# Output products summed over all heads in column tiles, their sums turned by VectorE out of PSUM

## The chip, the cores and the metric

The kernel runs on one core of a Trainium2 chip. The metric is the device time of one execution in microseconds; the time before is the median of three runs. TensorE (PE in the profile) multiplies, VectorE (DVE), ScalarE (ACT) and GpSimd (POOL) work on the results, and SyncE (SP) and GpSimd issue the DMA transfers.

## What is computed

A layer and all of its gradients. The rows x (2048 x 512) are normalized to xn; one branch is a recurrent attention over 64 segments of 32 rows, the other a dense layer with a squared ReLU. Cut to what matters here:

```python
for s in range(n_seg):                        # 64 segments
    h = concatenate([mem, xn[s]])             # 8 memory rows + 32 rows
    q, k, v = h @ Wq, h @ Wk, h @ Wv          # 32 heads of 128
    p = softmax(where(mask, q @ k.T * scale, -1e9))
    o = sum over heads of (p @ v) @ Wo        # 40 x 512
    mem = o[:8]                               # the next segment's memory
    outs.append(o[8:])
out = x + concatenate(outs) + dense(xn)
```

The outputs are `out` and, by the chain rule from `grad_out`, the gradients of x, the first memory, the four attention weights and the dense layer's parameters. The memory makes two chains: forward, segment after segment, and backward, from the last to the first.

## The kernel before

It runs in stages: the dense branch forward and backward with the normalization, the projections of the "left" rows, the forward chain, the attention gradients of the left rows together with weight gradients of the dense branch, the backward chain, and the weight gradients of the attention with the last input gradients. A step of a chain works on the 8 memory rows and the first 24 rows of a segment (32 rows in all); the other 8 rows of each segment, which feed no memory, are gathered over four segments into blocks of 32 "left" rows. There are 64 steps and 16 blocks.

TensorE's array is used in column tiles: four products of 32 columns of weights each (`tile_position=(0, 32 * g)`) stand beside each other, one for each of four groups of 8 heads. `proj` (L392) makes q, k and v so, `scores` (L432 for the mask, which is added by a product of the identity with `maskA`, and L437 for q k) and `outer` (L547, four row tiles) the attention itself, and `gather` (L460) the output: for every head a product of its 32 rows with 512 columns of Wo, summed over the 8 heads of a group into 32 of the 128 partitions of `ps_R`. The backward chain uses `gather` three times a step, with the gradients of v, k and q and the turned weights. Left rows have the same products: `G0` and `G1` forward (`ps_RL`), and `G0` to `I3` backward (L1166).

The sums over the four groups are still missing then. `ra` and `rb` copy `ps_R` to SBUF as float32 (one half on VectorE, one on ScalarE), `ta` and `tb` turn it by four TensorE products with a float32 identity (`turn_ops`, L469, into `ps_sum`), and reductions on VectorE add up the groups (`over_groups`, L482): `HT` writes the 8 memory rows as the next step's input (X forward, GT backward), `xt` the other rows to XT. For left rows `left_sums` (L476) does that. `flip` (L165) turns q and k, or the gradient of the output, by whole 128x128 transposes, and `left_rows` (L350) projects left rows of later blocks with full 128-column weights.

The order of all this is written out by hand. `F_ORDER` and `B_ORDER` are lists of short names, one string for each of the four steps of a block; `play` calls them in that order, and each engine gets its instructions in the order of these calls. A name with `L.` belongs to the left rows of a block; `+` and `-` move a name to the step (or block) before or after. `ENGS` says which engine a copy runs on. PSUM tiles of a chain come from four banks in turn (`big`, `tr`), and four more banks hold the `outer` results.

Of the kernel before, what the change touches and what calls it, by code (L numbers as in the profile page):

```python
# [12 lines left out]
P = 128  # L13
# [13 lines left out]
def kernel(  # L27
# [75 lines left out]
    HG = 4  # L103
# [247 lines left out]

    def keep_left(dN, q, t, g):

        dma(S_NL[4 * q:4 * q + 4, 32 * g:32 * g + 32, t, :].rearrange("b r c -> r b c"), dN[:])
# [68 lines left out]

    def kgr(ps):
        return ps[:].rearrange("p (k g r) -> p k g r", k=4, g=HG)

    def scores(sc, qT, kTs, h, mask):

        sc3 = sc[:, 0:4 * KW].rearrange("p (k n) -> p k n", k=4)
        if mask is not None:  # L430
            w = sum(n for _, n in kTs)
            nc.tensor.matmul(sc3[:, :, 0:w], lhsT=ident[:], rhs=mask[:, :, 0:w], start=True, stop=False, skip_group_check=True)  # L432
        for k in range(4):
            c = 0
            for kT, n in kTs:
                for g in range(HG):
                    nc.tensor.matmul(sc3[32 * g:32 * g + 32, k, c:c + n], lhsT=qT[:, 4 * h + k, g, :],  # L437
                                     rhs=kT[:, 4 * h + k, g, :], start=(mask is None), stop=True,
                                     tile_position=(0, 32 * g), skip_group_check=True)
                c += n  # L440
# [11 lines left out]

    def gather(R, XT, W, h, first, last):

        for k in range(4 * h, 4 * h + 4):
            for g in range(HG):
                x, o = W(g * KH + k), R[32 * g:32 * g + 32, :]
                if len(x.shape) == 3:
                    o = o.rearrange("p (a b) -> p a b", b=P)
                nc.tensor.matmul(o, lhsT=XT(k, g), rhs=x,  # L460
                                 start=(first and k == 4 * h), stop=(last and k == 4 * h + 3),
                                 tile_position=(0, 32 * g))

    def turn_ops(o, alloc, R4, st):

        def tT(c):
            if "T" not in st:
                st["T"] = alloc("ps_sum")
            nc.tensor.transpose(st["T"][:, c * P:(c + 1) * P], R4()[:, c * P:(c + 1) * P], identF[:])  # L469
        for h in range(2):  # L470
            o["t%s" % "ab"[h]] = lambda h=h: [tT(c) for c in (2 * h, 2 * h + 1)]

    def left_sums(XT, T):

        for c in range(DC):
            nc.vector.tensor_reduce(XT[:, c], T[:, c * P:(c + 1) * P].rearrange("p (g j t) -> p j t g", g=HG, j=SPB),  # L476
                                    axis=AX.X, op=ALU.add)

    def over_groups(out, T, rows):

        with nc.allow_low_precision(reason="summed in float32, rounded once on the way out"):
            nc.vector.tensor_reduce(out, T[:].rearrange("p (c g r) -> p c r g", c=DC, g=HG)[:, :, rows], axis=AX.X,  # L482
                                    op=ALU.add)
# [97 lines left out]
    def play(order, n, steps, lefts, step, blk, done=None):  # L581
# [22 lines left out]
        "tb ta L.E0 HT",  # L604
        "L.W1 L.ob0 L.out- k0mm L.oa0 L.oa1 L.ob1 q0mm soP- L.E1 q1mm k0ev k1mm q0ev k0fl xt- q1ev k1ev k0Te q0fl "
        "q0Te q1fl k1fl k1Te L.hs s0 mx0 sb0 q1Te s1 v0mm mx1 sb1 ex0 v0ev su0 rc0 pm0 L.lq+ L.lp ex1 tu0 v1mm "
        "soN- su1 L.otr rc1 pm1 tu1 w0 v1ev ob0 L.P2 oa0 L.X0 w1 L.lo ob1 g0 oa1 g1 soP rb L.P3 km L.t3 ra tb ta "
        "soN HT",
        "k1mm q0mm k0mm L.E3 L.E2 kl L.sx- xt- q0ev k1ev q1mm k0ev k0fl q0fl q1ev k0Te L.hl++ k1fl q0Te L.u3 k1Te "
        "q1fl s0 mx0 q1Te s1 sb0 mx1 sb1 ex0 L.ldL+ ex1 su0 rc0 pm0 tu0 v0mm su1 v0ev rc1 pm1 v1mm L.X1 w0 v1ev "  # L610
        "tu1 oa0 ld L.G1 w1 soV- ob0 L.t2 km ob1 oa1 L.mtr g0 g1 ra L.P5 soP rb L.E5 tb ta HT",
        "L.G0 k0mm xt- L.ra q0mm kl q1mm k1mm k0ev q0ev k0fl q1ev k1ev q0fl k0Te q1fl q0Te k1fl L.u2 s0 q1Te "
        "L.lv+ L.lb k1Te L.t1 L.ta s1 mx0 sb0 mx1 sb1 v0mm ex0 ex1 v0ev v1mm su0 rc0 pm0 v1ev L.mst L.tb tu0 su1 "
        "w0 rc1 ob0 L.P4 pm1 tu1 L.xt oa0 L.E4 w1 oa1 soV- soN- g0 ob1 g1 km rb soV ra kl+ L.S0+ tb ta L.X2 soP "
        "L.u1 HT xt L.mx0+ L.S1+ L.sb0+ k0mm+ L.mx1+ q0mm+ L.sb1+ k1mm+ q1mm+ q0ev+ k0ev+ k1ev+ ld q1ev+ soN "
        "L.ex0+ k0fl+ q0fl+ k1fl+ k0Te+ q1fl+ q0Te+ L.ex1+ q1Te+ k1Te+ s0+ mx0+ v0mm+ sb0+ L.t0 L.su1+ ex0+ L.lm+ "
        "su0+ km+ s1+ mx1+ sb1+ v0ev+ ex1+ v1mm+ L.P0+ rc0+ v1ev+ pm0+ tu0+ ld++ w0+ oa0+ su1+ rc1+ pm1+ ob0+ "
        "L.P1+ tu1+ w1+ ld+ ob1+ L.su0+ L.rc0+ L.pm0+ oa1+ L.u0 L.rc1+ g0+ L.pm1+ g1+ soV+ L.tu0+ rb+ L.tu1+ "
        "L.W0+ L.BT ra+ kl++")
    ENGS = on_engines(  # L620
        "L.E1 L.E2 L.E4 L.oa0 L.ob0 k0ev k1ev oa0 ob0 ob1 q1Te q1ev rb v0ev v1ev",
        "L.E0 L.E3 L.E5 L.oa1 L.ob1 L.pm0 L.pm1 L.ra k0Te k1Te oa1 pm0 pm1 q0Te q0ev ra")
    with sb("fw", 1) as fw, psum("fr", 4) as fr, psum("fpp", 1) as fpp, \
# [64 lines left out]
        def left(b):  # L688
# [27 lines left out]
            for p in range(2):  # L716
                def S_(p=p):
                    ps["s%d" % p] = big("ps_scL")
                    scores(ps["s%d" % p], B_["qL"], ((B_["kM"], NL), (B_["kL"], NL)), p, maskL)
# [26 lines left out]
            def ra():  # L746
                st["R4"] = fo.tile([P, D], F32, name="R4L", tag="R4s")
                ENGS["L.ra"](st["R4"][:], ps["R"][:])
            o["ra"] = ra
            turn_ops(o, big, lambda: st["R4"], st)  # L750
            o["xt"] = lambda: left_sums(B_["XT"][:, :, :, 0:M], st["T"])

# [5 lines left out]
            for i in range(PER):  # L758
# [5 lines left out]
                def P_(i=i, q=q, t=t, g=g, h=h):  # L764
                    ps["L", i] = big("ps_L")
                    left_rows(ps["L", i], lambda dc: XL1[:, dc, (q - 1) * P:q * P], t, g, h)
# [39 lines left out]
        def fwd(s):  # L806
# [30 lines left out]
            for t, u, n in ((1, 2, "k"), (0, 1, "q"), (2, 0, "v")):  # L837
                for p in range(2):
# [10 lines left out]
                    def fl_(n=n, p=p, u=u):  # L849
                        ps[n, p] = tr("ps_tr")  # L850
                        flip(ps[n, p], T["N"][:, u, HC[p]])
# [5 lines left out]
            for p in range(2):  # L857
                def S_(p=p):
                    ps["s", p] = big("ps_sc")
                    scores(ps["s", p], T["qT"], ((T["kT"], L),), p, maskA)  # L860
# [26 lines left out]
            def ra(h):  # L887
                if "R4" not in st:
                    st["R4"] = fo.tile([P, D], F32, name="R4", tag="R4s")
                c = slice(h * 2 * P, (h + 1) * 2 * P)  # L890
                ENGS["r%s" % "ab"[h]](st["R4"][:, c], ps["R"][:, c])
            o["ra"], o["rb"] = lambda: ra(0), lambda: ra(1)
            turn_ops(o, big, lambda: st["R4"], st)

            def HTf():
                if s + 1 < NSEG:
                    b1, j1 = divmod(s + 1, SPB)
                    over_groups(block(b1)["X"][:, :, j1 * SEG:j1 * SEG + M], st["T"], slice(0, M))
            o["HT"] = HTf
            o["xt"] = lambda: over_groups(B_["XT"][:, :, j, M:SEG], st["T"], slice(M, SEG))  # L900
# [12 lines left out]
        with tc.manual_schedule():  # L913
# [9 lines left out]
            after_o = {"L.ra": 6, "L.tb": 5, "L.xt": 5}  # L923
# [13 lines left out]
    with sb("la", 2) as la, sb("ls", 2) as ls, sb("lo", 1) as lo_, sb("wg", 2) as wg, psum("lpp", 1) as lpp, psum("lr", 4) as lr:  # L937
# [151 lines left out]
        "L.ko1 kg0 d41 qea0 L.G2 qeb0 tu1 qg0 kla0 qp1 klb0 L.I1 qea1 qeb1 kp1 qg1 keb1 kea1 klb1 kg1 rb ra L.H1 "  # L1089
        "tb kla1 vtr ta ldq HT",  # L1090
        "L.H2 o0mm L.ra1 vc- pb- o0ev o1mm L.ktr o0fl o0te o1ev vp0 ldk- xt- s0 L.kst d10 d20 vea vp1 d30 vla "
        "o1fl d40 vtr vlb vg0 veb kp0 vc tu0 vtr+ o1te ldp qp0 qeb0 s1 qea0 d11 d21 kea0 keb0 d31 vg1 qg0 kla0 "
        "klb0 d41 kg0 kp1 tu1 kea1 qp1 L.I3 keb1 qeb1 kg1 qea1 qg1 rb ra L.I2 L.vtr tb ta HT",
        "L.G3 o0mm ldn- ldk- L.ra2 o0ev kla1- o1mm o1ev ldp o0fl pb- xt- klb1- vp0 o0te s0 vea L.gs d10 vp1 vla "
        "d20 ldq- o1fl d30 d40 vlb vg0 kp0 veb tu0 o1te keb0 qp0 s1 qea0 klb0 vg1 kea0 kla0 pb d11 d21 kg0 L.sl- "
        "d31 vc d41 tu1 qeb0 kp1 qp1 keb1 qg0 qea1 L.gl+ kea1 kg1 qeb1 qg1 rb ra tb ta L.H3 kla1 HT",
        "klb1- o0mm o1mm L.vst o0ev o0fl o1ev L.ra3 xt- vp0 o1fl vtr ldn- o0te o1te vp1 ldp vea s0 L.ldt+ ldq- "
        "vla d10 L.qtr s1 d20 d30 d40 vc tu0 vg0 d11 veb vlb d21 L.I0+ L.ldv+ kp0 ldk- kla0 qp0 vg1 d31 kea0 keb0 "
        "d41 kg0 qea0 qeb0 qg0 tu1 kp1 klb0 qp1 kea1 L.vo1+ qeb1 L.G0+ pb keb1 qea1 kg1 qg1 kla1 L.vo0+ rb L.ldk+ "
        "L.ta L.tb tb ra ta L.lq+ HT L.H0+ L.ra0+ L.xt o0mm+ o1mm+ o0ev+ o1ev+ o0fl+ o0te+ L.qst vp0+ o1fl+ ldq "  # L1100
        "L.qo0+ klb1 s0+ vea+ L.ko0+ o1te+ vla+ d10+ d20+ d30+ vp1+ vlb+ d40+ ldn s1+ vg0+ kp0+ ldk veb+ d11+ "
        "d21+ xt ldn+ tu0+ keb0+ d31+ ldp+ L.G1+ vg1+ L.qo1+ qp0+ L.sx+ kea0+")
    ENGS = on_engines(
        "L.ra0 kea0 keb0 keb1 kla0 kla1 o0ev o1ev qea0 qea1 qeb0 rb vea veb vla vlb",
        "kea1 klb0 klb1 o0te o1te qeb1 ra")
    with sb("bq", 1) as bq, sb("bt", 1) as bt, sb("bs", 2) as bs, sb("be", 1) as be, psum("bpp", 1) as bpp, psum("br", 4) as br:
# [17 lines left out]
        def block(b):  # L1124
            if b not in blk:
# [3 lines left out]
                          "XT": (bt, [P, DC, SPB, SEG], F32), "R4": (bt, [P, D], F32)}  # L1129
# [7 lines left out]
        def left(b):  # L1137
# [19 lines left out]
            for i in range(4):  # L1157
                for x, nm in enumerate("GHI"):
                    def G_(i=i, x=x):
# [4 lines left out]
                        for m, (W, n, k) in enumerate(jobs[6 * i + 2 * x:6 * i + 2 * x + 2]):  # L1164
                            for g in range(HG):
                                nc.tensor.matmul(ps["R", i][32 * g:32 * g + 32, :].rearrange("p (a b) -> p a b", b=P),  # L1166
# [377 lines left out]
```

## Time and profile before

| | us |
|---|---|
| median of the runs (three) | 3063.05 |
| lowest and highest | 3062.07, 3064.35 |
| span of the profiled execution, first to last instruction | 3059.8 |
| window of the forward chain, 300 to 1173 | 873; TensorE busy 807.5, DMA share 0.66 |
| window of the backward chain, 1455 to 2410 | 955; TensorE busy 858.5, DMA share 0.70 |
| float32 products of L469, busy | 102.4 + 13.8 + 10.9 |
| groups of L460 products, busy | 146.7, 141.6, 133.4 (backward), 126.4, 33.5 (forward) |

The mean granted TensorE clock of the execution is 0.971. "Busy" is the time in which at least one instruction of a group ran; products overlap, so the busy time of a group can't be had from its mean and count. "Issue" as a releaser means that the engine waited for nothing that the profile shows. A line such as `128*32 128x512 bf16` is a product with weights of 128 rows and 32 columns and 512 columns of moving data.

### The profile page before, as it was taken

What the parts mean: (1) busy time and instruction counts of PE and PEld (TensorE: products, weight loads), DVE (VectorE), ACT (ScalarE), POOL (GpSimd) and SP (SyncE); (2) the same over time, 40 slices, a digit from 0 to 9 for tenths busy, and PEclk for the clock granted to TensorE, in tenths of its full rate; (3) what the DMA queues carried; (4) which work ended last, traced back from release to release, by engine and by line L of the source; (5) the groups of instructions that cost most, each with busy time, mean ns of one, the idle gap of its engine ahead of it and who ended that gap; (6) DMA issues with size and microseconds to landing.
All of it is one profiled execution on the core that took longest, in us unless ns stands there. A gap on an engine that the chain in (4) does not pass through costs nothing. (4 is left out here: it accounts for less than half of the span.)

```text
span 3059.8 us, 109712 instructions
## 1 busy us (share of the span) xinstructions
PE 2705.4 (88%) x48600; PEld 1386.8 (45%) x48600; DVE 1319.5 (43%) x3581; ACT 994.7 (33%) x2306; POOL 658.0 (22%) x1264
## 2 busy tenths in 40 slices
PE   8997899999999886877799899998989559999998
PEld 4453444444444444446444444444444224444443
DVE  5452566666666664334345444544545201100010
ACT  2422444444444444323333333333333101111111
POOL 0000000000000000113343433434343213322222
PEclk9998999999999998999999999999999879999999
DMA  9548375766767767777577676776777899898991
GB/s 257 185 146 250 101 188 161 189 181 172 190 168 182 165 157 192 229 230 220 149 173 174 190 187 164 177 203 169 176 200 175 238 192 217 194 211 207 204 207 39
DMA packets 794559, 566.78 MB, mean 185 GB/s; under 512 B 579409, under 2 KB 681570, under 8 KB 790754
## 3 DMA queue, kind: packets, MB, share of 16 engines
q1 hardware_dynamic: 748322, 430.47, 58.8%
q0 software_dynamic: 40528, 126.53, 13.5%
q8 instruction: 381, 6.24, 0.9%
q10 hardware_dynamic: 5232, 2.75, 0.4%
q14 instruction: 96, 0.79, 0.1%
HBM read 193.61 MB, written 238.56 MB: 141 GB/s over the span
## 5 line engine op out<-in xcount | busy, mean ns | idle before, releaser
L1505 PE MATMUL ps_gw<-gn,HNc 128*128 128x512 bf16 x1920 | 416.4, 379 | 0.0
L1505 PEld LDWEIGHTS <-HNc 128*128 128x128 bf16 x1920 | 187.8, 98 | 223.9
L374 ACT CAST f_N<-ps_proj 128x512 bf16<-128x512 f32 x320 | 185.9, 581 | 243.9 <-PE ps_proj L392 223.4
L1476 ACT CAST wt<-ps_gw 128x512 bf16<-128x512 f32 x128 | 74.4, 586 | 503.5 <-PE ps_gw L1505 474.4
L392 PEld LDWEIGHTS <-X 128*32 128x32 bf16 x6144 | 153.3, 97 | 161.3 <-DVE X L482 13.9
L835 POOL COPY kM<-f_kT 128x256 bf16<-128x256 bf16 x64 | 25.6, 401 | 786.7 <-DVE f_kT L377 594.9
L1459 DVE TENSOR_TENSOR gx<-ps_rows,gb 128x512 f32<-128x512 f32 x16 | 11.1, 692 | 420.5 <-PE ps_rows L1457 418.2
L1505 PE MATMUL ps_gw<-GOc,gn 128*128 128x512 bf16 x640 | 142.2, 385 | 54.8 <-DMA GOc<-S_GM 54.8
L460 PE MATMUL ps_gR<-Wk,gk 128*32 128x512 bf16 x2048 | 146.7, 386 | 19.4 <-ACT gk L374 12.9
L392 PE MATMUL ps_proj<-Wk,X 128*32 128x512 bf16 x2048 | 135.4, 384 | 12.6 <-DVE X L482 6.9
L460 PE MATMUL ps_gR<-Wq,gq 128*32 128x512 bf16 x2048 | 141.6, 382 | 1.2 <-issue 1.2
L374 ACT CAST gk<-b_pp 128x256 bf16<-128x256 f32 x192 | 68.8, 377 | 208.3 <-PE b_pp L547 146.6
L1477 POOL DMA_DIRECT2D out_dram<-wt x128 | 69.2, 541 | 309.5 <-ACT wt L1476 309.4
L1239 POOL COPY PD<-b_P 32x320 bf16<-32x320 bf16 x256 | 114.9, 449 | 95.3 <-PE b_pp L1292 64.4
L460 PE MATMUL ps_gR<-Wv,gv 128*32 128x512 bf16 x2048 | 133.4, 379 | 0.3 <-issue 0.3
L392 PE MATMUL ps_proj<-Wo,GT 128*32 128x512 bf16 x2048 | 123.9, 384 | 7.9 <-POOL GT L1203 6.7
L392 PE MATMUL ps_proj<-Wq,X 128*32 128x512 bf16 x2048 | 128.7, 382 | 0.0
L460 PE MATMUL ps_R<-Wo,OT 128*32 128x512 bf16 x2048 | 126.4, 388 | 0.0
L469 PE MATMUL ps_sum<-identF,R 128*128 128x128 f32 x512 | 102.4, 295 | 24.6 <-ACT R L374 18.4
L392 PE MATMUL ps_proj<-Wv,X 128*32 128x512 bf16 x2048 | 124.1, 378 | 0.0
L1505 PEld LDWEIGHTS <-gn 128*128 128x128 bf16 x640 | 63.4, 99 | 132.3 <-issue 59.6
L374 ACT CAST gON<-ps_proj 128x512 bf16<-128x512 f32 x128 | 74.9, 585 | 143.2 <-PE ps_proj L392 141.5
(260 smaller groups left out, 5128.0 us busy)
## 6 DMA issues: line engine op xcount, KB each, us to landing
S_A<-f_N SPq DMA_DIRECT2D x64, 512.0 KB
out_dram<-wt POOLq DMA_DIRECT2D x142, 128.0 KB, 4.6
S_A<-f_N SPq DMA_DIRECT2D x64, 256.0 KB
S_GB<-gv SPq DMA_DIRECT2D x32, 512.0 KB
S_GB<-gq SPq DMA_DIRECT2D x32, 512.0 KB
S_GB<-gk SPq DMA_DIRECT2D x32, 512.0 KB
b_kN<-S_A POOLq DMA_DIRECT2D x63, 256.0 KB, 5.0
b_qN<-S_A POOLq DMA_DIRECT2D x63, 256.0 KB, 5.4
```

What stands on the lines that cost most here:

```text
L374: nc.scalar.copy(out, in_)
L392: nc.tensor.matmul(o, lhsT=hT[:, dc, :], rhs=x, start=(dc == 0), stop=(dc == DC - 1), tile_position=(0, 32 * g))
L460: nc.tensor.matmul(o, lhsT=XT(k, g), rhs=x, start=(first and k == 4 * h), stop=(last and k == 4 * h + 3), tile_position=(0, 32 * g))
L469: nc.tensor.transpose(st["T"][:, c * P:(c + 1) * P], R4()[:, c * P:(c + 1) * P], identF[:])
L835: o["km"] = lambda: nc.gpsimd.tensor_copy(B_["kM"][:, :, :, lc], T["kT"][:, :, :, 0:M])
L1239: nc.gpsimd.tensor_copy(PD[32 * g:32 * g + 32, g], C["P"][32 * g:32 * g + 32, :, 0:L])
L1459: nc.vector.tensor_tensor(out=gx[:], in0=ps[:], in1=gb[:], op=ALU.add)
L1476: nc.scalar.copy(wt[:], ps[:])
L1477: pdma(dst, wt[:])
L1505: nc.tensor.matmul(ps[:], lhsT=l(rc), rhs=r(rc), start=(n == 0), stop=(n == RC_ALL - 1))
```

## The change

`gather` and the left rows' products now call `columns_of`: for each head four products, each with all of the head's 32 rows and 128 of the 512 columns (32 out of every 128), on the four column tiles. All 32 heads are summed in PSUM, and `ps_R` holds 128 x 128 sums. A single 32x32-block transpose on VectorE (`RT`) brings them out of PSUM, already turned, to XT; `HT` copies the 8 memory rows from there. The copies `ra`/`rb`, the TensorE turns `ta`/`tb` and the reductions `xt`, `over_groups` and `left_sums` are gone. In the forward chain the turns of q and k (`flip_tiles`), the masks and the left projections (`left_tiles`) are done in four column tiles as well, and the mask covers only the columns that it can change. The backward flips stay whole. `HT` is a VectorE copy in both chains; in the backward chain XT has two buffers, and a memset of its memory rows is dropped.

```diff
+    def left_tiles(ps, x, t, g, h):
+        c0 = g * GW + h * 512
+        for dc in range(DC):
+            for c in range(4):
+                nc.tensor.matmul(ps[32 * c:32 * c + 32, :], lhsT=x(dc)[:, 32 * c:32 * c + 32], rhs=Wqkv[t][:, dc, c0:c0 + 512],
+                                 start=(dc == 0), stop=(dc == DC - 1), tile_position=(0, 32 * c))
...
+    def flip_tiles(ps, srcN):
+        for k in range(4):
+            for c in range(4):
+                nc.tensor.transpose(ps[32 * c:32 * c + 32, k * P:(k + 1) * P], srcN[:, k * P + 32 * c:k * P + 32 * c + 32],
+                                    ident[:], tile_position=(0, 32 * c))
...
-            w = sum(n for _, n in kTs)
-            nc.tensor.matmul(sc3[:, :, 0:w], lhsT=ident[:], rhs=mask[:, :, 0:w], start=True, stop=False, skip_group_check=True)
+            m, lo, hi = mask
+            for c in range(4):
+                nc.tensor.matmul(sc3[32 * c:32 * c + 32, :, lo:hi], lhsT=ident[:, 32 * c:32 * c + 32], rhs=m[:, :, lo:hi],
+                                 start=True, stop=False, tile_position=(0, 32 * c), skip_group_check=True)
...
+    def columns_of(R, XT, W, first, last):
+        x = W if len(W.shape) == 3 else W.rearrange("p (a b) -> p a b", b=P)
+        for c in range(HG):
+            nc.tensor.matmul(R[32 * c:32 * c + 32, 0:P].rearrange("p (a b) -> p a b", b=32), lhsT=XT,
+                             rhs=x[:, :, 32 * c:32 * c + 32], start=first, stop=last, tile_position=(0, 32 * c))
+
     def gather(R, XT, W, h, first, last):
         for k in range(4 * h, 4 * h + 4):
             for g in range(HG):
-                x, o = W(g * KH + k), R[32 * g:32 * g + 32, :]
-                if len(x.shape) == 3:
-                    o = o.rearrange("p (a b) -> p a b", b=P)
-                nc.tensor.matmul(o, lhsT=XT(k, g), rhs=x,
-                                 start=(first and k == 4 * h), stop=(last and k == 4 * h + 3),
-                                 tile_position=(0, 32 * g))
+                columns_of(R, XT(k, g), W(g * KH + k), first and k == 4 * h and g == 0, last and k == 4 * h + 3 and g == HG - 1)
...
 F_ORDER, second step (end)
-        "soN- su1 L.otr rc1 pm1 tu1 w0 v1ev ob0 L.P2 oa0 L.X0 w1 L.lo ob1 g0 oa1 g1 soP rb L.P3 km L.t3 ra tb ta "
-        "soN HT",
+        "L.otr rc1 pm1 tu1 w0 v1ev ob0 L.P2 oa0 L.X0 w1 L.lo ob1 g0 oa1 g1 soP L.P3 km L.t3 RT HT soN",
 B_ORDER, second step (end)
-        "klb0 d41 kg0 kp1 tu1 kea1 qp1 L.I3 keb1 qeb1 kg1 qea1 qg1 rb ra L.I2 L.vtr tb ta HT",
+        "kp1 tu1 kea1 qp1 L.I3 keb1 qeb1 kg1 qea1 qg1 RT HT L.I2 L.vtr",
...
+            o["RT"] = lambda: nc.vector.transpose(B_["XT"][:, :, j, :], ps["R"][:, 0:P])
             def HTf():
                 if s + 1 < NSEG:
                     b1, j1 = divmod(s + 1, SPB)
-                    over_groups(block(b1)["X"][:, :, j1 * SEG:j1 * SEG + M], st["T"], slice(0, M))
+                    ENGS["HT"](block(b1)["X"][:, :, j1 * SEG:j1 * SEG + M], B_["XT"][:, :, j, 0:M])
...
-            o["xt"] = lambda: left_sums(B_["XT"][:, :, :, 0:M], st["T"])
+            o["RT"] = lambda: nc.vector.transpose(B_["XT"][:, :, :, 0:M], ps["R"][:, 0:P])
...
-                if j == SPB - 1:
-                    nc.gpsimd.memset(B_["XT"][:, :, :, 0:M], 0.0)
```

## The prediction

> **What bounds the kernel now.** I read the page first (busy shares, then the DMA queues), then the groups by line for TensorE, then the timeline around one turn of the forward chain, then the waits of the backward stage, and last the packed trace, record by record, for what one merged line hides. The first line gives busy time, share and instructions of TensorE; the two queue lines say what one queue carries.
>
> ```profile
> PE 2705.4 (88%) x48600; PEld 1386.8 (45%) x48600; DVE 1319.5 (43%) x3581; ACT 994.7 (33%) x2306; POOL 658.0 (22%) x1264
> ...
> q8 instruction: 381, 6.24, 0.9%
> ...
> q14 instruction: 96, 0.79, 0.1%
> ```
>
> TensorE is in use nearly always, but in the two chains it isn't full. A forward step takes 13.6 us (63 distances between the L482 reductions that write X: 870 us in all) and a backward step 14.8 us. One turn of the forward chain shows where the order of dependent work stands: start, duration, engine, line.
>
> ```profile
> 395.25 1.91 PE L460 MATMUL ps_R<-Wo,OT 128*32 128x512 bf16 x32
> ...
> 397.21 0.42 DVE L377 COPY R<-ps_R 128x256 f32<-128x256 f32 x1 [1.38 <-PE ps_R L460]
> 397.73 0.37 ACT L374 COPY R<-ps_R 128x256 f32<-128x256 f32 x1 [1.90 <-DVE R L377]
> 398.15 0.42 PEld L469 LDWEIGHTS ps_sum<-identF,R 128*128 128x128 f32 x4 [0.52 <-ACT R L374]
> 398.15 0.66 PE L469 MATMUL ps_sum<-identF,R 128*128 128x128 f32 x4
> ...
> 398.85 0.29 DVE L482 TENSOR_REDUCE X<-ps_sum 128x32 bf16<-128x128 f32 x1
> ```
>
> After the last output product the sums are copied by two engines, one after the other, turned by four float32 products and reduced; only then may the next step's projections start. From the last output product's start to the first projection's the packed trace has 2.41, 2.19, 2.83 and 2.19 us for the four steps of a forward block (mean 2.41; 0.6 to 1.7 us of it is other useful work), and 2.19 us for each backward one.
>
> The second bound is easily missed. In the backward stage TensorE stops for up to 2.8 us with no releaser (waits by engine and line: us in total, times, longest):
>
> ```profile
> PEld L547 <- issue: 108.4, 209, 2.8
> ...
> PE b_pp L547 <- issue: 11.6, 5, 2.7
> ```
>
> ```profile
> 1512.93 0.18 PE L547 MATMUL b_pp<-gST,b_kN 32*128 32x32 bf16 x1
> 1515.09 0.19 PE L547 MATMUL b_pp<-gST,b_kN 32*128 32x32 bf16 x3 [1.98 <-issue]
> ```
>
> The two lines are the timeline across one of them. The stop falls in the middle of a run of equal products. In the packed trace 13 such stops in this stage, 19.1 us together, lie at one place: TensorE's own row number, counted from the start, leaves 192 or 193 when divided by 256. TensorE has 97,535 rows there and q8 brought 381 packets of 16,384 bytes, so a packet is 256 rows of 64 bytes: TensorE's program. Each packet starts only around the row where the previous block is entered (39 rows before it to 256 behind it), so just one block is on its way. In 12 of the 13 stops TensorE goes on 2.2 to 2.5 us after the latest packet's start; the packet took 0.9 to 1.2. And from the entry of a block to the start of the next packet it is, in 8 of 10 cases, 0.4 to 1.6 us (median 0.9) where the DMA engines were under 30% busy in the 2.5 us before, 0.5 to 3.4 (median 1.8) where they were over 95% busy, and 1.2 to 6.3 (median 2.95) behind the 13 stops. So a block can't be replaced in less than about 0.9 + 2.3 = 3.2 us; the shortest distance between two packets in the whole run is 3.28 us. Today a block lasts 873/145 = 6.0 us in the forward and 955/170 = 5.6 us in the backward stage (windows 300 to 1173 and 1455 to 2410 us), so the limit is seldom touched.
>
> **The change part by part.** Products, by shape. Each output product of 512 columns becomes four of 128. Four neighbours on four column tiles run together: the x32 line above is 8 such groups, (1.91 - 0.39)/7 = 217 ns a group. A group of 128 columns isn't in this trace; the nearest rows are transposes of 128 columns, 56 ns from start to start, and four-tile score products of 40 columns (L437), 25 ns a group. I take 56, which is nearest in columns; the bounds are that 25 and the 70 ns of a 160-column product (L1290). 2,560 groups of 216 become 10,240 of 56: 553 to 573 us, +8 ns per old group: +0.06 us a forward step (8 groups), +0.24 a backward step (24 of the step, 6 of the block). At 70 ns it would be 143 us more by products alone, but 256 rows would still need only 2.2 us. All 640 float32 products of L469 go (102.4 + 13.8 + 10.9 us busy), with the copies (0.42 and 0.37) and the reductions (0.29 and 0.55).
>
> The chain behind the last output product becomes: product 0.22 (mean of the 128-column transposes), hand-over 0.06, RT on DVE, hand-over 0.04, HT, hand-over 0.06. RT (float32 128x128 from PSUM, turned) has no row: between the reduction of 128x128 (0.27) and the bf16 transpose of 128x256 (0.445); I take 0.30, since it reads as many elements as the reduction. HT (32 elements) lies between the reciprocal (0.18) and the reduction (0.29): 0.20. Sum 0.87 us (0.83 to 1.10). Beside it TensorE now has, in the four forward positions, one left projection (0.92), that and L.G0 (1.83), the left scores (0.67), and W0, BT and W1 with the casts between (1.58, from the same jobs at 424.8 us). The larger of chain and cover: 0.92, 1.83, 0.87, 1.58, mean 1.30 instead of 2.41: -1.11. Without its cover a position costs 0.87. Backward, the covers are two left jobs (0.95) or one (0.88 by the chain), mean 0.92 instead of 2.19: -1.27.
>
> Flips and masks in column tiles: the stop between projection and flip (312 ns against 213 for the product alone) loses 0.10 us a step; 16 groups of 56 replace 16 transposes of 56. Between mask and score the copies of q and k end last (DVE f_qT, 0.27 us of waiting), so that drain was covered and brings nothing; at most 0.2 us in one position of four. Left projections change 4 x 216 for 4 groups of 216.
>
> The added wait is RT's for the last output product. Behind it on DVE stand HT, dN casts and L.out, or in the backward order L.xt and o0te; only HT has someone waiting (the next projection), and it is in the chain above. L.RT waits for L.G0, which is ahead of the projections anyway. No DMA is issued elsewhere; POOL loses a memset per block.
>
> So by products and chain alone: forward 13.6 - 1.11 - 0.10 + 0.06 = 12.45 us, backward 14.8 - 1.27 + 0.24 = 13.8.
>
> Program rows. Added products: 30,720 by the outputs, 3,072 by flips, 480 by masks, 792 by left projections, 640 gone: +34,424, each with its weight load, so 166,400 rows and 650 packets. Forward: +11,704 products; (37,080 + 23,408)/64 = 945 rows, 3.7 blocks a step. Backward: +22,720; (43,536 + 45,440)/64 = 1,390 rows, 5.43 blocks. Its 128-product runs ask for 256 rows in 1.8 us. The densest 128 products of this trace took 2.84 us, so that pace was never tried. The price of a block that is waited for lies between 3.2 us (above) and 2.95 + 2.4 = 5.4 us (behind the stops). The same bytes over a longer stage would lower the DMA share of the backward stage from 0.70 to about 0.5, which puts it half-way between a free queue (3.2) and a loaded one (1.8 to 2.95 plus 2.4, middle 4.7): 3.9 us.
>
> Backward every block is dense: 5.43 x 3.9 = 21.2 us, +6.4 a step, 64 steps: +410 us. Forward two of 3.7 blocks hold the 512-column projections and the softmax waits and last over 3.9 on their own; the other 1.7 need 1.7 us each, and the first of them is often already fetched, so 1.2 stops of 2.2 us: 12.45 + 2.6 = 15.1, +1.5 x 64 = +96. The rest of the span (ffn, left back, weight gradients) is untouched. 3059.8 + 506 = 3566 us of span; the median of the runs, 3063.05, is 3.2 above the span: about 3570 us.
>
> [...]
>
> **The rivals.** *The program keeps up* (0.10): packets start earlier than in this trace once rows are short, or more than one is under way. Then forward -1.15 x 64 = -74, backward -1.0 x 64 = -66: 2925 us, faster. For it: today 51 of 64 backward steps have no stop, and the densest rows of this trace never asked for more; against it: 13 stops of one kind, and never under 3.28 us between packets. It decides below 2.7 us a block, where 12.45 + 1.2 (c - 1.7) + 5.43 c equals 28.4. *Nearly* (0.07): 2.7 to 3.1 us a block, 3065 to 3225 us, typically 3120. *Loaded queue* (0.11): the median behind the stops, 5.4 us: backward 29.3 (+930), forward 3.7 x 5.4 = 20 (+410): about 4400 us. A sag of TensorE's clock would push there too: the window 2410 to 2468 us, nearly idle, shows 0.58.
>
> **How the numbers follow.** The forecast, 3.1 to 4.75 us a block, has 0.72. At 3.1: backward 16.8 (+130), forward 14.1 (+34), 3225 us; at 4.75: 25.8 (+705) and 17.6 (+256), 4025 us. With the nearest part of both neighbours the range is 3200 to 4050. About 0.2% is what a measurement of this kernel can tell from no change. Faster by more than that: the first rival and an edge of the second, 0.11; within: 0.01; slower: 0.88.
>
> **What would show it.** Right: q8 with some 650 packets, 3.5 to 4.5 us apart in the backward stage; L469 gone; stops named "issue" in the middle of output products, about 1 to 2 us each; RT near 0.30 and HT near 0.20 us. Wrong: output groups of 128 columns running at 56 ns with no stop at every 256th row, or a step under 13 us.

## The result, and the profile after

| us | before | after |
|---|---|---|
| median of the runs | 3063.7 | 3684.07 (3678.58 to 3688.45) |
| ratio | 1 | 1.203, 95% interval 1.200 to 1.205 |
| span of the profiled execution | 3059.8 | 3678.1 |
| forward chain, mean distance of steps | 13.63 | 15.89 |
| backward chain, mean distance of steps | 14.86 | 22.43 |

The 63 forward distances grew by 142.0 us in all, the 63 backward ones by 476.6, and the left rows' stage and the end by 1.3 and 0.4; the start shrank by 2.1. These add up to the 618.3 us by which the span grew, so the whole loss lies in the two chains.

The page after, busy times, granted clock (tenths in 40 slices) and the two instruction lines of the queues (packets, MB, share):

```profile
PE 2846.7 (77%) x83024; PEld 1880.6 (51%) x83024; DVE 1194.0 (32%) x3341; ACT 946.0 (26%) x2177; POOL 657.7 (18%) x1248
...
PEclk9989999999998989887788878888888877999999
...
q8 instruction: 650, 10.65, 1.2%
...
q14 instruction: 91, 0.75, 0.1%
```

TensorE is busy a little longer than before but a smaller share of the time, VectorE less, and q8 brings the 650 packets that the prediction counted. The clock is the line that its sum did not count: 0.7 and 0.8 through most of the second chain. The windows of the chains, before and after (us; busy PE, PEld, DVE, ACT, POOL; clock, DMA share, GB/s):

```profile
314.00:1173.00 859.00, 796.66 (x18328) 409.02 (x18324) 554.85 (x1593) 376.87 (x851) 50.07 (x125) 1.00 0.67 170
1458.00:2414.00 956.00, 861.52 (x21821) 440.63 (x21814) 464.37 (x1324) 343.22 (x976) 364.54 (x703) 0.99 0.70 178
```

```profile
312.00:1312.00 1000.00, 796.69 (x29752) 520.99 (x29737) 499.32 (x1470) 354.50 (x787) 50.33 (x125) 0.95 0.61 147
1599.00:3032.00 1433.00, 990.57 (x44098) 807.41 (x44099) 393.85 (x1208) 317.66 (x911) 362.78 (x687) 0.83 0.46 121
```

One turn of the backward chain after (start, duration, engine, line):

```profile
2204.64 0.66 PE L474 MATMUL ps_gR<-Wq,gq 128*32 128x128 bf16 x16
...
2205.07 1.09 PE L474 MATMUL ps_RL<-Wq,b_gqL 128*32 128x128 bf16 x32
2205.36 0.32 DVE L1315 STREAM_TRANSPOSE b_XT<-ps_gR 128x128 f32<-128x128 f32 x1 [8.86 <-PE ps_gR L474]
2205.71 0.18 DVE L385 CAST GT<-b_XT 128x32 bf16<-128x32 f32 x1
...
2205.94 2.68 PE L400 MATMUL ps_proj<-Wo,GT 128*32 128x512 bf16 x32
```

The order of dependent work is as short as it was meant to be: RT 0.32, HT 0.18, then the projection. But the 32 projection products take 2.68 us here, at a granted clock of 0.71, where 32 products of this shape took 1.91 us in the turn shown of before, at 1.00. What eats the gain stands in the waits (of the whole run: us in total, times, longest) and in the timeline across one stop:

```profile
PEld L474 <- issue: 451.4, 274, 4.7
...
PE ps_gR L474 <- issue: 257.4, 151, 4.5
...
PEld L545 <- issue: 177.1, 309, 2.8
```

```profile
2213.36 0.85 PE L474 MATMUL ps_gR<-Wv,gv 128*32 128x128 bf16 x47
2217.20 0.44 PE L474 MATMUL ps_gR<-Wv,gv 128*32 128x128 bf16 x17 [2.99 <-issue]
```

A run of 64 equal products is cut after the 47th for 2.99 us, and nothing that the profile shows released it. In the packed trace (stops of over 0.5 us, from one row's start to the next) 258 of the backward stage's 345 blocks begin with such a stop, 450.9 us in all, and 113 of the forward stage's 235, 168.5 us; nine in ten of TensorE's gaps of over 1 us lie at its row 193 modulo 256. Before, these were 14 (20.2 us) and 2 (1.3 us). So the stops grew by 431 and 167 us, where the two chains grew by 477 and 142.

### The profile page after: what moved, and what is told of

Read it like the earlier page. It is cut to its first block, busy times and chain, and to the rows that moved or that the text cites. A ratio compares the mean times of both kernels' runs of the same rounds, so it can differ in the third digit from the quotient of the medians.

```text
span 3678.1 us, 178065 instructions
## 1 busy us (share of the span) xinstructions
PE 2846.7 (77%) x83024; PEld 1880.6 (51%) x83024; DVE 1194.0 (32%) x3341; ACT 946.0 (26%) x2177; POOL 657.7 (18%) x1248
## 4 chain that ended last, share of the span: by engine, by line
PE 47%; issue 12%; DMA 3%; DVE 3%; ACT 1%; SPq 1%; POOL 0%; POOLq 0%; DVEq 0%; ACTq 0%
PE ps_gw L1474 15%; PE ps_gR L474 13%; PE ps_proj L400 5%; PE ps_RL L474 3%; PE b_pp L545 3%; PE ps_w L1029 1%; PE ps_w L1023 1%; PE ps_tr L165 1%; PE ps_sc L454 1%; PE b_pp L1272 1%; DMA wB<-S_AN 1%; DMA wB<-S_GH1N 1%; ACT gk L382 0%; DMA gn<-S_OL 0%; PE ps_R L474 0%
## 5 line engine op out<-in xcount | busy, mean ns | idle before, releaser
L474 PE MATMUL ps_gR<-Wk,gk 128*32 128x128 bf16 x8192 | 216.1, 271 | 107.8 <-issue 92.8
L474 PE MATMUL ps_gR<-Wq,gq 128*32 128x128 bf16 x8192 | 210.4, 267 | 107.9 <-issue 107.5
L400 PEld LDWEIGHTS <-X 128*32 128x32 bf16 x6144 | 175.5, 100 | 178.1 <-issue 54.3
L474 PEld LDWEIGHTS <-gk 128*32 128x32 bf16 x8192 | 180.0, 124 | 124.8 <-issue 104.8
L474 PEld LDWEIGHTS <-gq 128*32 128x32 bf16 x8192 | 178.7, 123 | 122.7 <-issue 121.4
L474 PE MATMUL ps_R<-Wo,OT 128*32 128x128 bf16 x8192 | 155.9, 236 | 68.1 <-issue 67.8
L1445 ACT CAST wt<-ps_gw 128x512 bf16<-128x512 f32 x128 | 74.5, 587 | 487.3 <-PE ps_gw L1474 478.8
L474 PE MATMUL ps_gR<-Wv,gv 128*32 128x128 bf16 x8192 | 149.2, 223 | 57.1 <-issue 57.1
L474 PEld LDWEIGHTS <-OT 128*32 128x32 bf16 x8192 | 134.7, 105 | 79.4 <-issue 77.1
L400 PE MATMUL ps_proj<-Wo,GT 128*32 128x512 bf16 x2048 | 147.7, 426 | 24.6 <-issue 12.7
L474 PEld LDWEIGHTS <-gv 128*32 128x32 bf16 x8192 | 122.1, 98 | 66.9 <-issue 63.0
```

The source lines that it names most:

```text
L400: nc.tensor.matmul(o, lhsT=hT[:, dc, :], rhs=x, start=(dc == 0), stop=(dc == DC - 1), tile_position=(0, 32 * g))
L474: nc.tensor.matmul(R[32 * c:32 * c + 32, 0:P].rearrange("p (a b) -> p a b", b=32), lhsT=XT, rhs=x[:, :, 32 * c:32 * c + 32], start=first, ...
L1445: nc.scalar.copy(wt[:], ps[:])
```

## The experiments

The theory under test is that of the prediction: TensorE's program comes in blocks of 256 rows (97,535 rows and 381 packets in the trace before, 166,382 and 650 after), a dense block can't be had in less than about 3.9 us, and the change adds rows. The rivals: the 128-column products are slow in themselves (array, PSUM, clock); the new turn or the column tiles of the turns cost the time. Steps are the mean distances in the profiled run of each kernel, as in the table.

**The new chain with the old products.**

```diff
-    for c in range(HG):
-        nc.tensor.matmul(R[32 * c:32 * c + 32, 0:P]..., rhs=x[:, :, 32 * c:32 * c + 32], ...)
+    nc.tensor.matmul(R[32 * g:32 * g + 32, :]..., rhs=x, ..., tile_position=(0, 32 * g))
```

> The changed kernel with its output products put back to one of 512 columns per head (four groups of heads on four column tiles): about 104,960 TensorE rows and 410 packets on q8 instead of 650. RT, HT, the orders, and the column tiles for forward turns, masks and left projections stay. Left out: the sum over the four groups and three quarters of the output columns. Program theory (dense blocks of 256 rows take 3.85 us): the chain's saving comes out without its price, forward steps near 12.5 us, backward steps near 13.8 us, 2920 us (2880 to 2970). Rival 'the turn on VectorE or the column tiles of the turns are what is slow': not under 3063 us. Rival 'the 128-column products are slow in themselves': as the program theory here, the next kernel tells them apart.

Measured: 2990.52 us, ratio 0.976 (0.973 to 0.980), steps 12.87 and 14.32 us, 410 packets. Its backward window:

```profile
1416.00:2338.00 922.00, 805.16 (x21508) 422.19 (x21508) 392.72 (x1214) 317.39 (x912) 362.99 (x687) 0.98 0.75 185
```

The turn, the copy and the column tiles of the turns are not what is slow: with them, and with 240 packets fewer than after, the kernel is faster than before. It is 70 us slower than was expected, and outside the range of that expectation; where this went is told below.

**The same rows, a quarter of the columns, then twice the columns.**

```diff
-            nc.tensor.matmul(R[32 * c:32 * c + 32, 0:P] ..., rhs=x[:, :, 32 * c:32 * c + 32], ...)
+            nc.tensor.matmul(R[32 * c:32 * c + 32, 0:32 * n] ..., rhs=x[:, 0:n, 32 * c:32 * c + 32], ...)   # n: 4 for the first product, then 1
...
+            nc.tensor.matmul(R[32 * c:32 * c + 32, 0:2 * P] ..., rhs=x[:, :, 64 * (c // 2):64 * (c // 2) + 64], ...)   # the second kernel
```

> The changed kernel with the same products and weight loads, 166,400 rows and 650 packets, but every output product except the first of a sum has 32 columns instead of 128 (three quarters of the columns keep only the first head: left out). Program theory: the same blocks must come, so nearly the same time, 3640 us (3580 to 3690), stops at the same row of every block and longer, since the products are shorter. Rival 'the 128-column products are slow (array time, PSUM or clock)': 10,240 groups of four at 25 ns instead of 56, so about -317 us, 3370 us or less.

> The changed kernel with every output product twice as long: 256 columns instead of 128 into twice the PSUM columns, the same 166,400 rows and 650 packets. RT reads the first 128 of the 256, which are not the wanted ones: left out is the right choice of columns. Program theory: 32 groups of 256 rows now ask for 32 x 112 = 3.6 us where a waited block takes 3.85 us, so the doubled array time fits into the stops, and the granted clock rises from 0.83 as TensorE idles less: 3690 us (3600 to 3770). Rival 'product time counts': +10,240 groups x 56 ns = +573 us, 4260 us.

Measured: 3775.05 us with 32 columns (ratio 1.233, 1.228 to 1.237), 3723.62 with 256 (1.212, 1.210 to 1.214), against 3684.07 with 128. Eight times the columns move the time by 51 us, and in the other direction. Of each kernel a group of output products (count | busy, mean ns | idle before) and the backward window, 32 columns first, then 256:

```profile
L475 PE MATMUL ps_gR<-Wq,gq 128*32 128x32 bf16 x8192 | 103.7, 192 | 197.3 <-issue 197.0
```

```profile
1635.00:3127.00 1492.00, 780.89 (x44144) 556.84 (x44146) 392.84 (x1208) 317.00 (x911) 361.36 (x686) 0.65 0.46 116
```

```profile
L475 PE MATMUL ps_gR<-Wq,gq 128*32 128x256 bf16 x8192 | 269.8, 277 | 55.4 <-issue 55.2
```

```profile
1610.00:3078.00 1468.00, 1233.36 (x44098) 1049.50 (x44095) 396.14 (x1208) 317.72 (x911) 361.99 (x686) 0.98 0.47 118
```

What the products gain in busy time, the stops take, and the other way round: TensorE is busy 781 us in one window and 1233 in the other, and the windows are 1492 and 1468 us long. The stops at block borders sum to 679 us backward with 32 columns, 450.9 with 128 and 234.3 with 256. The rival of slow products falls. So does the clock as the main cause: with 256 columns it is granted at 0.98, and the step (22.98 us) is no shorter than at 0.83 (22.43), where the slower groups are 2.2 us of array time (worked out below) against the 7.6 us by which the step grew. The kernel with 256 columns came within its expectation; the one with 32 missed it, 3775 against at most 3690. Its clock is 0.65, and its 512-column projections from GT take 601 ns in the mean, 426 in the changed kernel. The added time lies in the backward blocks without a stop, most of which hold such products: 75 of 5.2 us in the mean, against 87 of 4.5 in the changed kernel; blocks with a stop last 4.1 in both.

**Rows alone, on the kernel before.** Products of 4 columns of zeros are added to the same sums, with the old chain.

```diff
+        def zeros(k):
+            for _ in range(n):                    # n = 1, then n = 3
+                for g in range(HG):
+                    nc.tensor.matmul(R[32 * g:32 * g + 32, 0:4], lhsT=XT(k, g), rhs=zero4[:], start=False, stop=False, ...)
```

> The kernel before with one more product of 4 columns of zeros for each output product, added to the same sums (the result does not change): 118,015 rows, 461 packets. Old chain, old turns. Program theory: a stage pays only where 256 rows ask for less than 3.85 us; with 512-column products between them a group of eight products takes about 242 ns, so 256 rows take 3.9 us, just at the limit: only the array time is added, 2,560 groups of 25 ns = 64 us, 3125 us (3080 to 3220). Rival 'every added product has its price, whatever the blocks': a third of what three zeros add. Rival 'rows cost nothing': 3063 to 3127 us.

> The kernel before with three more products of 4 columns of zeros for each output product: 158,975 rows, 621 packets. Old chain, no 128-column products, no new turn. Program theory: backward 5.47 blocks a step at the 4.18 us a block that the changed kernel shows = 22.9 us (+515 us), forward 3.2 blocks, +1.5 to +2.3 us a step (+100 to +150): 3700 us (3600 to 3800), with the stops at the same row of each block, and more than three times the loss of one zero. Rivals 'columns' and 'chain': only the array time of 7,680 groups of 25 ns, +192 us at most, 3255 us.

Measured: 3248.39 us with one (ratio 1.061, 1.054 to 1.067) and 3748.99 with three (1.224, 1.213 to 1.235). Without any part of the change, three zeros cost as much as the change and more: 621 packets, steps of 15.82 and 23.72 us. Of its 347 backward blocks 222 begin with a stop, 367 us in all, at the same row of the block as after; the zeros' own array time, at most 192 us by the expectation, and the lower clock (0.87) are in the loss too and were not taken apart. The backward window, and one line of the zeros:

```profile
1599.00:3113.00 1514.00, 1145.54 (x44410) 674.51 (x44411) 459.90 (x1313) 343.19 (x974) 365.23 (x702) 0.87 0.45 115
```

```profile
L460 PE MATMUL ps_gR<-zero,gk 128*32 128x4 bf16 x6144 | 124.0, 171 | 64.4 <-issue 64.2
```

The expectation for one zero was missed, 3248 against at most 3220. It took all blocks as alike. The trace has 88 backward blocks with a stop, about 133 us or 2.1 us a step (0.3 before), where that step grew by 2.57; and the median block with a stop lasts 4.4 us, not 3.9, at a higher DMA share (0.61). So the price begins with the densest blocks and isn't a threshold of the mean: one zero costs 186 us and three 687, 3.7 times as much. That was expected to be far more uneven.

**The column tiles of the turns undone.**

```diff
-                        flip_tiles(ps[n, p], T["N"][:, u, HC[p]])
+                        flip(ps[n, p], T["N"][:, u, HC[p]])
...
-                    left_tiles(ps["L", i], ...)
+                    left_rows(ps["L", i], ...)
```

> The changed kernel with the forward turns of q and k, the masks and the left projections put back to whole products: 8,688 TensorE rows fewer (nearly all in the forward chain, 136 a step, 0.53 block), output products, RT and HT as changed. Program theory: the forward chain stops at 113 of its blocks and these rows are dense (64 products in 0.9 us), so most of 0.53 x 4.1 us comes back: -0.5 to -1.5 us a step, 3590 to 3650 us; backward unchanged at 22.4 us a step. Rival 'column tiles for the turns pay by the drain they save': +0.1 us a step, 3684 to 3695 us.

Measured: 3673.08 us, ratio to before 1.196 (1.191 to 1.200), just below the 1.203 of the changed kernel and above the expected 3590 to 3650 us. The forward step falls by 0.81 us to 15.08, as expected; the column tiles of the turns, with their 136 rows a step, cost more than the wait that they shorten: from projection to turn it was 312 ns before and 192 in the median after. But the backward step, whose code is the same and which was expected unchanged, rose from 22.43 to 23.01 us and took 37 us of it back. Its added time is in stops that end 2.1 to 3.3 us behind a packet (492.6 us against 456.0). Why the same code stops longer there stays open.

**Can the short chain be had without the rows?** First a mixture: wide products for most heads, whose sums ScalarE copies and a float32 selector (128x32, ones where the row within a group matches) adds up in PSUM, and 128-column products for the last 16, 8 or 0 heads.

```diff
+        R4 = alloc4()
+        acp(R4[:], ps["Ra"][:])                  # sums of the wide products, 128x512
+        jobs = [(XT(k, g), W(g * KH + k)) for k in range(4 * h + 4 - NC, 4 * h + 4) for g in range(HG)]
+        jobs.insert(12 if NC == 4 else len(jobs), (sel[:], R4[:]))
+        for i, (w, x) in enumerate(jobs):
+            columns_of(ps["R"], w, x, i == 0, i == len(jobs) - 1)
```

> A mixture on the kernel before: all output products but the last half of the last gather stay 512 columns wide on four groups; their sums are copied by ScalarE alone (128x512) and added over the groups by four float32 products with a 128x32 selector into the same PSUM tile as the last 16 heads, which come in 128-column products; then RT and HT as in the change. About 109,800 rows (+96 a step). Left rows, turns and masks as before. Program theory: the chain's saving seen with wide products (-0.77 us forward, -0.54 backward) less the selector (0.35) and less 0.375 block a step (0.3 to 0.8 us): between 3030 and 3110 us, 3070. Rival 'rows cost nothing, only the chain counts': 2990 to 3010 us.

> The same mixture with only the last 8 heads in 128-column products: +48 rows a step, about 103,700 rows. The ScalarE copy (0.58 us) is then not quite covered by 0.45 us of products, and the selector comes last. Program theory: the chain from the last wide product to the next projection is 2.06 us where it was 2.62, less 0.2 to 0.4 us for 0.19 block: 3020 to 3070 us, 3045. Rival 'rows cost nothing': 3000 us.

> The same mixture with no 128-column heads at all: the wide sums are copied by ScalarE alone, added and regrouped by the four selector products, turned by VectorE. No rows more than before (97,500). Program theory: no block is added, the chain behind the last output product is 0.39 + 0.06 + 0.58 + 0.04 + 0.35 + 0.06 + 0.32 + 0.03 + 0.18 + 0.05 = 2.06 us less the 0.17 that a product's end overlaps, against 2.19 to 2.41: -0.2 to -0.4 us a step, 3010 to 3040 us, 3025. Rival 'the saving came from the short chain alone, and this one is as long': 3063 us.

Measured: 3101.4 us (ratio 1.011, 1.007 to 1.014), 3081.1 (1.0025, 1.0001 to 1.0049) and 3107.17 (1.012, 1.007 to 1.016). The first is within its expectation, the second just above, the third far off. With no 128-column products TensorE waits for the copy, since the selector stands ahead of the products that covered the copies before:

```profile
2002.61 0.58 ACT L384 COPY R<-ps_gR 128x512 f32<-128x512 f32 x1 [1.78 <-PE ps_gR L520]
...
2003.25 0.43 PE L474 MATMUL ps_gR<-R,sel 128*32 128x128 f32 x8 [0.73 <-ACT R L384]
2003.34 0.57 SPq L1181 DMA_DIRECT2D S_GM<-GT  x1
2003.37 0.54 POOL L1274 DMA_DIRECT2D b_qN<-S_A  x1
...
2003.49 1.05 PE L1199 MATMUL ps_RL<-Wq,b_gqL 128*32 128x512 bf16 x16
```

The covering products of left rows start at 2003.49, behind the wait of 0.73 us. The expectation had left the queue's order out of the sum.

Then two kernels without any added product row for the chain, both on the kernel before:

```diff
-                c = slice(h * 2 * P, (h + 1) * 2 * P)
-                ENGS["r%s" % "ab"[h]](st["R4"][:, c], ps["R"][:, c])
+                c = slice(64 * h, 64 * h + 64)
+                ENGS["r%s" % "ab"[h]](st["R4"][c, :], ps["R"][h][c, :])      # two banks, copied side by side
...
+            nc.tensor.matmul(R()[0][:, c * 32:c * 32 + 32], lhsT=R4()[:, c * P:(c + 1) * P], rhs=sel[:], ...)
...
+                acp(st["R4"][:], ps["R"][:])                                 # the other kernel: one copy by ScalarE
```

> The kernel before with a shorter chain and no added row (one output tile split over two banks by head groups, so that ScalarE and VectorE copy 64 partitions each side by side, 0.69 and 0.58 us, instead of one after the other, 0.42 + 0.10 + 0.37; four float32 products with a 128x32 selector, which add up the groups, instead of four turns of 128 columns, 0.57 for 0.66; and a copy of 0.18 instead of the reduction of 0.29): the chain behind the last product 1.56 us instead of 1.93. Program theory: no block is added, so up to 0.37 us a step stays, less where useful work covers it: 3015 to 3050 us, 3030. Rival 'the chain is covered by other work or the loads end last': 3060 us. Rival 'an additional bank in the rotation of four makes steps wait': over 3070 us.

> The kernel before with the copy of the output sums done by ScalarE alone (128x512, 0.58 us) where two engines copied one half each, one after the other (0.42 + 0.10 + 0.37 us). No row, no product, no block is added. Program theory: the 0.3 us stay wherever no product covers the copy: most backward steps (cover 0.44 us or none), few forward ones (cover 0.92 us); -20 to -30 us: 3035 us (3025 to 3060). Rival 'ScalarE comes late with its other casts, or the turn of the first half now waits': 3070 us or more.

Measured: 3138.51 us (ratio 1.022, 1.020 to 1.023) and 3068.46 (0.9996, 0.998 to 1.001). In the first one the copies do run side by side, but the selector is dearer than the turns that it replaces:

```profile
2007.90 0.68 DVE L379 COPY R<-ps_gR 64x512 f32<-64x512 f32 x1 [1.09 <-PE ps_gR L462]
...
2007.99 0.58 ACT L376 COPY R<-ps_gR 64x512 f32<-64x512 f32 x1 [1.44 <-PE ps_gR L462]
...
2008.72 1.05 PE L484 MATMUL ps_gR<-sel,R 128*128 128x32 f32 x8 [0.43 <-DVE R L379]
```

Four selector products are eight in the records and take 1.05 us; the four float32 turns of 128 columns took 0.66. That is 0.39 us of the 0.7 by which the backward step grew; the rest was not followed up. The expectation (3015 to 3050 us) failed, and its rival of the additional bank, over 3070, is not excluded: no kernel tried the bank alone. In the second, which also missed its range, the chain behind the last backward product went only from 2.19 to 2.16 us. The packed trace shows why (medians, counted from that product's start, the turns in three of the four positions). The one copy ends at 1.07 us, where the second of the two had ended at 1.31. But before, two of the four turns began at 0.91, beside that second copy; now all four wait for the whole copy, and the last one begins at 1.51 instead of 1.53. That is the rival which the expectation named. No version tried here that keeps all of the sums is faster than the kernel before.

## Why the prediction was right

The forecast, slower at 3570 us within 3200 to 4050, held: 3684. Its mechanism is shown by three kernels: rows without the change bring the loss (three zeros), the change without its rows is faster than before (wide products), and the products' length hardly matters (32 and 256 columns). Step by step:

**The price of a block.** 3.9 us forecast, 3.91 measured as the median of the 258 backward blocks with a stop (3.84 if stops from 0.3 us on are counted): 1.41 us from entry to packet (about 1.5 was assumed) and 2.43 from packet to resumption (2.4). The rival of the program that keeps up falls, with its 2925 us. The prediction read the trace before a little too evenly: the 14 stops counted there now last 0.7 to 2.8 us and not all over 2, 11 of them end 2.2 to 2.5 us behind a packet and three 3.4 to 3.5, and the wait ahead of the packet is 0.6 to 3.8 us (median 3.1).

**Backward, 5.43 x 3.9 = 21.2 us.** Measured 22.43. The price was right for the typical block with a stop, but two things are missing. The blocks with a stop are uneven, and their mean is 4.08 us. And not every block is dense, as the sum had it: the 87 without a stop last 4.47 us by themselves. Each makes about half of the difference, and the mean over all 345 is 4.17, which gives 5.4 x 4.17 = 22.5. This is most of what the forecast lacked: 1.2 us x 64 = 79 us.

**Forward, 12.45 + 1.2 stops of 2.2 us.** Measured 1.77 stops a step of 1.49 us: 2.63 against 2.64, but that is luck, since more stops came and each was shorter. The base was low: 15.89 - 2.63 = 13.26 us instead of 12.45. Of these 0.8 us the groups of 128 columns can explain about half: they took 65.4 ns in the mean, 9 more than assumed, times 40 a step, 0.38 us. The rest was not traced.

**The chain.** 0.87 forecast. In the backward stage the medians are 0.22 for the product, 0.04, RT 0.317, 0.034, HT 0.182 and, at two of the four positions, 0.05 to the projection's start: 0.85. At the other two the projection waits for covers or stops. The covers held too: with wide products, 0.16 us longer than the 0.22, the four forward positions measure 1.91, 1.07, 1.93 and 1.02 us (mean 1.48; 1.30 + 0.16 was the sum), the backward ones 1.01 to 1.07 (0.92 + 0.16). Yet that kernel's backward step gained 0.54 us and not 1.15. The stall went elsewhere, which the sum had not asked: stops at block borders grew from 20.2 to 38.5 us (0.29 a step), and the waits of TensorE's weight loads for the transfer of `b_qN` from 2.8 to 19.5 us (0.26 a step). The line in the backward window before, and then in that kernel's (busy, mean ns | idle before):

```profile
L547 PEld LDWEIGHTS <-b_qN 32*128 32x128 bf16 x2048 | 37.0, 91 | 65.6 <-issue 61.0 <-DMA b_qN<-S_A 2.8
```

```profile
L545 PEld LDWEIGHTS <-b_qN 32*128 32x128 bf16 x2048 | 36.8, 91 | 76.2 <-issue 55.7 <-DMA b_qN<-S_A 19.5
```

**The groups of 128 columns.** Forecast 56 ns, and 56 is the median. The clock was the term that was missing (the prediction names a sag beside the loaded queue alone, without a price): 35% of the backward groups took about 106 ns (mean 74.5). In the trace after they go with the clock: in the backward window the groups that start where it was granted at 1.0 took 56 ns in the median, those that start where it was granted at 0.5 took 107. By 120 groups a step it is 2.2 us of array time, but most of it lies where a block is waited for anyway: with 256 columns a group takes 113 ns in the mean, 4.6 us a step more, and the step is only 0.55 us longer.

**The other rivals.** The loaded queue (5.4 us a block) did not come: from entry to packet it was 1.41 us and not 2.95, at a DMA share of 0.46, about the 0.5 that the sum assumed. The nearly fast program falls with the price of 3.91. The 0.10 us that the flips in column tiles were to save is swamped: undoing them gained 0.81 us a forward step.

## What to carry to other kernels

Count program rows next to array time: a product split into four is four products and four weight loads to fetch (here 166,382 rows in 650 packets where 97,535 had come in 381). In this kernel a block of 256 rows that was waited for took 3.91 us in the median, and where the rows asked for less, the fetch set the pace nearly whatever the products' length (3775, 3684 and 3724 us with 32, 128 and 256 columns). A stop with no releaser in the middle of equal instructions, at a fixed row number (here 193 of 256), is how that looked in the trace; adding rows that do nothing (three zeros: 3749 us) and changing the length of products at equal rows told it apart from slow products. A shorter dependent chain is worth only what the next limit leaves (with wide products 0.54 us of 1.15 a backward step), so ask of each saved microsecond which transfer or block is due next.

## What had not been expected of the hardware

Stops of 1 to 3 us, one per block, went with a lower granted clock: 0.83 in the backward window, 0.65 when the products between them were shorter still, 0.98 when they were longer, at the same rows. The wait from the entry of a block to its successor's packet follows the DMA share in most kernels: among blocks with a stop its backward median is 3.33 us at a share of 0.75 (wide products), 1.87 at 0.61 (one zero) and 1.41 at 0.46 (after), though 1.75 at 0.47 (256 columns); from packet to resumption it was 2.41 to 2.53 us in all of these. Float32 products against a selector were recorded twice each (eight records of four), where the float32 turns were recorded once (four of four). The two copies of `ps_R` ran one after the other before, and out of two banks side by side, but that says nothing of the banks: before, the profile names the first copy as the releaser of the second (`<-DVE R L377`), a wait of the program, and in the split kernel both are released by TensorE (`<-PE ps_gR L462`).
